# Two left half passes in every segment, and left output rows placed from scratch memory

## The chip, the core and the metric

The kernel runs on one core of a Trainium2 chip. A core has a matrix engine (TensorE, PE), a vector engine (VectorE, DVE), a scalar engine (ScalarE, ACT), a general engine (GpSimd, POOL) and an engine that mainly issues transfers (SyncE, SP). They run side by side and meet through semaphores. Sixteen DMA engines move data between the chip's main memory (HBM) and the on-chip memory, and work off what SP and POOL issue. TensorE writes its sums into accumulator banks, which another engine empties. The metric is device time in microseconds (us), lower is better.

## What is computed

Two branches work on the same layer-normed input and are added to it: a recurrent attention with memory (A), and a dense layer with GELU (B). Sizes: 2048 rows of 1024; 32 heads of 128; segments of 32 rows, so 64 segments; 8 memory rows; hidden width 3584.

```python
def _A_ref(x, mem0, Wq, Wk, Wv, Wo, seg_len):
    ...
    for s in range(n_seg):
        xs = x[:, s * seg_len:(s + 1) * seg_len, :].copy()
        h = jnp.concatenate([mem, xs], axis=1)
        q = jnp.einsum('btd,dhe->bhte', h, Wq)
        k = jnp.einsum('btd,dhe->bhte', h, Wk)
        v = jnp.einsum('btd,dhe->bhte', h, Wv)
        scores = jnp.einsum('bhqe,bhke->bhqk', q, k) * scale
        scores = jnp.where(mask[None, None], scores, -1000000000.0)
        p = _softmax(scores, axis=-1)
        o = jnp.einsum('bhqk,bhke->bhqe', p, v)
        o = jnp.einsum('bhte,hed->btd', o, Wo)
        mem = o[:, :M, :].copy()
        outs.append(o[:, M:, :])
    return jnp.concatenate(outs, axis=1)
...
xn = _layernorm(x, axis=-1)
return x + _A_ref(xn, A_mem0, A_Wq, A_Wk, A_Wv, A_Wo, A_seg_len) + _B_ref(xn, B_w1, B_b1, B_w2, B_b2)
```

The first 8 output rows of a segment are the memory rows of the next one, so the 64 segments run one after another, and each uses all of Wq, Wk, Wv and Wo.

## The kernel before

**First part.** For four blocks of 512 rows the kernel does the layer norm, the dense layer and the sum with x (lines 214 to 453). The sum, R_n, goes to main memory; turn_R (L309) rearranges it there into hr_d (for each segment) and hrL_d (for each group of four), in the layout in which the attention output will come. The normed rows go there too, transposed, in columns 0 to 255 of the same two tensors.

**Main rows and left rows.** A product with a weight uses at most 32 rows at a time. Of the 40 rows of a segment, 8 memory rows and the first NX = 24 rows of x are the main rows. The other NL = 8 are the left rows. As they don't depend on the recurrence until the attention, the left rows of four segments (GRP = 4, a group) are put together to 32 and go through the weights once for each group. In segment s, g, i4 = divmod(s, GRP).

**Weights.** Wq, Wk, Wv and Wo are cut into 64 units of 128 x 2048 elements, 512 KB each. 43 stay in on-chip memory; 21, spread evenly over the order of use, are fetched again in each segment (IS_STREAMED, "the stream"). They go through STREAM_BUFS = 6 buffers on SP's queue: start_stream (L182) issues the next transfer, and is called by unit_done (L480) when a streamed unit has been used; the transfer waits until TensorE has read the buffer. unit_done also hands one or two of the waiting small transfers (the list named small) to POOL's queue.

**A segment** (L508 to L787) is a fixed order of half passes. half_pass (L526) multiplies eight units of K, Q or V (u = 0 or 1, half of the heads) with the main rows into an accumulator, and, if asked (left), with the left rows into a second one, psL. Dictionaries named at say after which unit other work is done: turning keys and queries (turn_k, turn_q, and turn_kL, turn_qL for left rows), scores, sums (the softmax denominators) and values. The order is K0, Q0, V0, K1, Q1, V1, then the output product with 16 units of Wo (o_product, L672), where a left output product from the tiles oL goes into psXL. There are three accumulator banks in turn, named acc. K0 is called with lead=3: products of left rows with up to three resident units come before the first main product.

Before, the left half passes stand so: K0, K1 and V1 in segments with i4 = 0; none with i4 = 1; Q0 and Q1 with i4 = 2; V0 and the output product with i4 = 3 (left_k, left_q, left_v and left_o, lines 518 to 521). The output product takes as many matrix instructions as two half passes. Values VL[u] of left rows, keys kL[u] and queries qL are kept over the segments of a group; qS (L703) keeps the queries for the last segment while qL is written for the next group.

**End of a segment.** ScalarE copies the output sum to o_sb (L768). put_mem (L204) turns it on TensorE, and VectorE copies the 8 memory columns into the next segment's hT (L208). On VectorE the order is: with i4 = 3, resL = psXL + resL (L771); then the memory copy L208; then res = psX + res (L774). res and resL come by POOL from hr_d and hrL_d after unit 7 of the output product (L762, L765). Four stores of res (L778) and, with i4 = 3, 16 stores of resL (L785) are appended to small. The softmax tile pr and res share one piece of on-chip memory (tag "e"), resL shares one with VL[1] (tag "VL1").

**Queues.** [...] On POOL these are, for a segment: hr for the next segment (L194, waits until TensorE has used the present one, after V1), res, resL, then the stores. SP has the stream alone once the first segment has started.

Of the kernel before, what the change touches and what calls it, by code (L numbers as in the profile page):

```python
# [10 lines left out]
BF16 = mybir.dt.bfloat16  # L11
# [5 lines left out]
P = 128  # L17
# [6 lines left out]
SEG = 32  # L24
MEM = 8
NSEG = S // SEG
# [9 lines left out]
NX = 24  # L36
NL = SEG - NX
# [36 lines left out]
def kernel(  # L74
# [34 lines left out]
    hr_d = dram.tile([NSEG + 1, P, 512], BF16, name="hr_d")  # L109
    hrL_d = dram.tile([NGRP + 1, P, 512], BF16, name="hrL_d")  # L110
    R_n = dram.tile([S, DM], BF16, name="R_n")

    slabs = ctx.enter_context(tc.tile_pool(name="slabs", bufs=1))
    consts = ctx.enter_context(tc.tile_pool(name="consts", bufs=1))
# [100 lines left out]
    with tc.tile_pool(name="ma", bufs=2) as ma, tc.tile_pool(name="mps", bufs=6, space=PSUM) as mps:  # L215
# [93 lines left out]
        def turn_R(ttg, small=None):  # L309

            for i in range(4):
                rows = R_n[ttg * P + i * SEG:ttg * P + (i + 1) * SEG, :].rearrange("t (j c) -> t j c", j=4)
                dst = hr_d[4 * ttg + i + 1, :, 256:512].rearrange("(j t) c -> t j c", j=4)
                dstL = hrL_d[ttg + 1, :, 256:512].rearrange("(j t) c -> t j c", j=4)[NL * i:NL * i + NL, :, :]
                for o, r in ((dst, rows), (dstL, rows[NX:SEG, :, :])):
                    if small is None:
                        nc.sync.dma_start(out=o, in_=r)
                    else:
                        small.append(lambda o=o, r=r: nc.gpsimd.dma_start(out=o, in_=r))
# [140 lines left out]
    with tc.tile_pool(name="late", bufs=1) as late, \  # L460
# [43 lines left out]

        hT, hL = nxt["hT"], nxt["hL"]
        qL = qlp.tile([P, 8, P], BF16, name="qL")
        kL, VL, oL = [None] * 2, [None] * 2, [None] * 2
        for s in range(NSEG):  # L508
            g, i4 = divmod(s, GRP)
            first, final = s == 0, s + 1 == NSEG  # L510
# [3 lines left out]
                small.appendleft(lambda g=g: load_left_rows(g + 1, nc.gpsimd))  # L514


            more = g + 1 < NGRP
            left_k = i4 == 0
            left_q = first or (i4 == 2 and more)
            left_v = first or (i4 == 3 and more), i4 == 0  # L520
            left_o = i4 == 3
            if left_q and not first:
                hL = nxt["hL"]
            st = {}
# [37 lines left out]
            def left_out(psL, tag, pool=sp):  # L562
                nat = pool.tile([P, 512], BF16, name="natL", tag=tag)
                nc.vector.tensor_copy(out=nat[:, :], in_=psL[:, :])  # L564
                return nat

            def turn_k(nat):
                tr = trp.tile([P, 4, P], BF16, name="tr")
# [16 lines left out]
            def turn_qL(nat, u):  # L585
                turn4(nat, qL[:, 4 * u:4 * u + 4, :])

            def q_left(u):

                if i4 == 3 and more:  # L590
                    q = qS[:, u, :, :]
                else:
                    q = by_head(qL[:, 4 * u:4 * u + 4, :])[:, :, NL * i4:NL * i4 + NL]
                nc.vector.tensor_copy(out=st["qT"][:, :, 32:40], in_=q)
# [51 lines left out]
            def values(u, r):  # L646

                V, prA, prB = st["V"], st["prA"], st["prB"]
                av = avp.tile([P, 2, 512], F32, name="av")
                oV = av[:, :, 0:160].rearrange("p b (c q) -> p b c q", q=40)  # L650
                for c in range(4):
                    for b in range(2):
                        q = slice(64 * r + 32 * b, 64 * r + 32 * b + 32)
                        nc.tensor.matmul(  # L654
                            oV[:, b, c, :], lhsT=V[q, c * P:(c + 1) * P], rhs=prA[q, c, :],
                            start=(c == 0), stop=False, skip_group_check=True, tile_position=(64 * r + 32 * b, 0),
                        )
                    for b in range(2):
                        q = slice(64 * r + 32 * b, 64 * r + 32 * b + 32)
                        nc.tensor.matmul(  # L660
                            oV[:, b, c, NX:40], lhsT=VL[u][q, c * P:(c + 1) * P], rhs=prB[q, c, :],
                            start=False, stop=True, skip_group_check=True, tile_position=(64 * r + 32 * b, 0),
                        )
                if r == 0:
                    st["oT", u] = sp.tile([P, 4, 4, 32], BF16, name="oT", tag="db"[u])
                    if i4 == 0:
                        oL[u] = late.tile([P, 4, 4, 32], BF16, name=f"oL{u}")
                cp = nc.vector.tensor_copy if r else nc.scalar.copy
                cp(out=st["oT", u][:, 2 * r:2 * r + 2, :, :], in_=oV[:, :, :, 0:32])  # L669
                cp(out=oL[u][:, 2 * r:2 * r + 2, :, NL * i4:NL * i4 + NL], in_=oV[:, :, :, 32:40])  # L670

            def o_product(unit, t, lhs, acc, seq):  # L672
                w, i, u = unit
# [22 lines left out]
                at[2].append(lambda: q_left(0))  # L696
            if left_q:
                at[2].append(lambda: st.update(natL=left_out(psQL, "d")))
                at[5] = [lambda: turn_qL(st["natL"], 0)]
                if first:  # L700
                    at[5].append(lambda: q_left(0))
                else:
                    qS = sp.tile([P, 2, 16, NL], BF16, name="qS")  # L703
                    at[5].insert(0, lambda: keep_q(0))
            psV, psVL = half_pass("V", 0, left_v[0], at)
            st["V"] = left_out(psV, "b")
            if first:
                VL[0] = left_out(psVL, "VL0", late)


            psK1, psK1L = half_pass("K", 1, left_k, {1: [sums]})
            natk1 = rows_out(psK1, "d")
            at = {2: [lambda: turn_k(natk1)], 4: [lambda: values(0, 0)], 6: [lambda: values(0, 1)]}
            if left_k:
                at[2].append(lambda: st.update(natL=left_out(psK1L, "d")))
                at[4].insert(0, lambda: turn_kL(st["natL"], 1))
            psQ1, psQ1L = half_pass("Q", 1, left_q, at)
            natq1 = rows_out(psQ1, "b")
            if left_v[0] and not first:
                VL[0] = left_out(psVL, "VL0", late)  # L720
            at = {3: [lambda: turn_q(natq1)], 6: [lambda: scores(1)]}
            if first:
                at[3].append(lambda: st.update(natL=left_out(psQ1L, "VL1", late)))
# [3 lines left out]
            if left_o:  # L727
                psXL = accp.tile([P, 512], F32, name="acc")

                def o_lefts(k):
                    for unit in O_LEFT[k]:
                        o_product(unit, unit_tile(unit), oL, psXL, O_LEFT_SEQ)

                at.setdefault(1, []).append(lambda: o_lefts(0))
            psV1, psV1L = half_pass("V", 1, left_v[1], at)
            st["V"] = left_out(psV1, "a")
            if left_v[1]:
                VL[1] = left_out(psV1L, "VL1", late)  # L740
            if not final:
                load_x_rows(s + 1, nc.gpsimd)


            at = {1: [sums], 4: [lambda: values(1, 0)], 6: [lambda: values(1, 1)]}
            if left_q and not first:
                at[7] = [lambda: keep_q(1)]
                at[8] = [lambda: st.update(natL=left_out(psQ1L, "d"))]
                at[11] = [lambda: turn_qL(st["natL"], 1)]
            psX = accp.tile([P, 512], F32, name="acc")  # L750
            resL = None
            for n, unit in enumerate(O_UNITS):
                t = unit_tile(unit)
                o_product(unit, t, [st["oT", 0], st.get(("oT", 1))], psX, O_UNITS)
                if left_o and unit in O_LEFT[1]:
                    o_product(unit, t, oL, psXL, O_LEFT_SEQ)
                unit_done(unit)
                for fn in at.get(n, ()):
                    fn()
                if n == 7:  # L760
                    res = sp.tile([P, 256], BF16, name="res", tag="e")
                    nc.gpsimd.dma_start(out=res[:, :], in_=hr_d[s + 1, :, 256:512])  # L762
                    if left_o:
                        resL = late.tile([P, 256], BF16, name="resL", tag="VL1")
                        nc.gpsimd.dma_start(out=resL[:, :], in_=hrL_d[g + 1, :, 256:512])  # L765
            if not final:
                o_sb = sp.tile([P, 256], BF16, name="o_sb", tag="d")
                nc.scalar.copy(out=o_sb[:, :], in_=psX[:, 0:256])  # L768
            if left_o:
                o_lefts(2)  # L770
                nc.vector.tensor_tensor(out=resL[:, :], in0=psXL[:, 0:256], in1=resL[:, :], op=ALU.add)  # L771
            if not final:
                put_mem(o_sb, nxt["hT"], trp.tile([P, 4, P], BF16, name="tr"))
            nc.vector.tensor_tensor(out=res[:, :], in0=psX[:, 0:256], in1=res[:, :], op=ALU.add)  # L774

            for jq in range(4):
                o = out_flat[s * SEG:s * SEG + NX, 256 * jq:256 * jq + 256]
                small.append(lambda o=o, r=res[32 * jq:32 * jq + NX, :]: nc.gpsimd.dma_start(out=o, in_=r))  # L778
            if left_o:
                rows_o = out_flat[g * GRP * SEG:(g + 1) * GRP * SEG, :].rearrange("(i t) d -> i t d", t=SEG)  # L780
                for jq in range(4):
                    for i in range(GRP):
                        o = rows_o[i, NX:SEG, 256 * jq:256 * jq + 256]
                        r = resL[32 * jq + NL * i:32 * jq + NL * i + NL, :]
                        small.append(lambda o=o, r=r: nc.gpsimd.dma_start(out=o, in_=r))  # L785
            if not final:
                hT = nxt["hT"]  # L787
# [35 lines left out]
```

The softmax here doesn't subtract the row's maximum and nothing guards it: scores larger than these inputs give would overflow.

## Time and profile before

| What | us |
|---|---|
| Runs (four): lowest, median, highest | 2338.39, 2346.52, 2351.84 |
| The profiled execution, its own time | 2338.39 |
| Its span in the trace | 2336.6 |
| TensorE busy (share of the span) | 2023.7 (87%) |
| VectorE busy | 699.0 (30%) |
| ScalarE busy | 517.3 (22%) |
| POOL busy | 372.7 (16%) |
| First o_sb copy (end of segment 0) begins | 472.3 |
| Last o_sb copy (end of segment 62) begins | 2285.9 |

The profiled execution is the fastest of the four runs. Its span is 1.8 us shorter than its time. Busy shares are means over unlike stages: the first part is 420 us of matrix work with little traffic, and the 64 segments after it move 512 KB units all the time. The queue of SP moved 769.66 MB in all, that of POOL 15.92 MB. In the chain of waits that ended last, 50% of the span is TensorE and 40% is transfers, most of these the stream: 24% waiting for units of Wq, 5% each for Wo and Wv, 3% for Wk.

Among the transfers of POOL, res takes 5.2 us from issue to landing in the median, the stores of res 5.2 us and of resL 5.4 us, hr 5.5 us, resL 5.1 us. A stream unit takes 6.6 to 7.4 us, of which several are under way at once.

### The profile page before, as it was taken

How to read it: one execution, taken by the hardware profiler on the slowest of the kernel's cores; microseconds unless marked ns; L12 is line 12 of the kernel's file. 1: busy time of each engine (PE TensorE's matmuls, PEld its weight loads, DVE VectorE, ACT ScalarE, POOL GpSimd, SP SyncE). 2: the span in 40 equal slices, each digit the busy share in tenths (PEclk: the TensorE clock that was granted, in tenths of full speed). 3: DMA queues.
4: the chain of work that ended last, by engine and by line, in shares of the span. 5: the costliest groups of instructions: out<-in, count | busy, mean ns of one | idle time of the engine just before them, and what ended most of it. 6: DMA issues, size and time to landing. Idle time of an engine off the chain costs nothing.

```text
span 2336.6 us, 84620 instructions
## 1 busy us (share of the span) xinstructions
PE 2023.7 (87%) x37779; PEld 1046.7 (45%) x37779; DVE 699.0 (30%) x1922; ACT 517.3 (22%) x1221; POOL 372.7 (16%) x745
## 2 busy tenths in 40 slices
PE   7999999788888888888888888888888888888885
PEld 3444444344444444444444444444444444444443
DVE  6574753122222222222222222222222222222221
ACT  5261432121212121211121111111212121111121
POOL 0000000023121212121212121212121212121212
PEclk9999999999999999999999999999999999999998
DMA  9521126899999999999999999999999999999995
GB/s 322 192 68 47 39 66 257 328 403 380 405 378 397 380 397 377 405 378 380 368 405 369 395 376 404 376 404 378 404 378 400 376 400 358 399 371 396 373 402 225
DMA packets 266409, 792.03 MB, mean 339 GB/s; under 512 B 55995, under 2 KB 71131, under 8 KB 266044
## 3 DMA queue, kind: packets, MB, share of 16 engines
q1 hardware_dynamic: 243004, 769.66, 85.4%
q0 software_dynamic: 22464, 15.92, 2.2%
q8 instruction: 295, 4.83, 0.8%
q10 hardware_dynamic: 576, 1.05, 0.1%
q14 instruction: 70, 0.57, 0.1%
HBM read 772.83 MB, written 29.88 MB: 344 GB/s over the span
## 4 chain that ended last, share of the span: by engine, by line
PE 50%; DMA 40%; issue 4%; DVE 3%; ACT 2%; POOL 1%; DVEq 0%; ACTq 0%; POOLq 0%; SPq 0%
DMA u<-Wc_Q 24%; PE acc L536 17%; PE ps L358 8%; PE acc L676 8%; PE ps L405 6%; DMA u<-Wc_O 5%; DMA u<-Wc_V 5%; DMA u<-Wc_K 3%; PE av L654 2%; PE tr L493 2%; DMA resL<-hrL_d 2%; PE ps L438 2%; PE av L660 1%; DMA res<-hr_d 1%; DVE natL L564 1%
## 5 line engine op out<-in xcount | busy, mean ns | idle before, releaser
L536 PE MATMUL acc<-u,hr 128*32 128x512 bf16 x12288 | 952.1, 384 | 133.9 <-DMA u<-Wc_Q 63.7
L536 PEld LDWEIGHTS <-hr 128*32 128x32 bf16 x12288 | 314.5, 96 | 471.6 <-issue 222.8
L536 PE MATMUL acc<-u,hrL 128*32 128x512 bf16 x3072 | 299.7, 381 | 4.0 <-ACT xtok L451 1.1
L559 ACT CAST nat<-acc 128x512 bf16<-128x512 f32 x256 | 150.1, 586 | 544.5 <-PE acc L536 506.2
L676 PEld LDWEIGHTS <-oT 128*32 128x32 bf16 x8192 | 208.6, 97 | 96.7 <-issue 76.8
L676 PE MATMUL acc<-u,oT 128*32 128x256 bf16 x4096 | 187.5, 275 | 22.8 <-DMA u<-Wc_O 11.2
L564 DVE CAST natL<-acc 128x512 bf16<-128x512 f32 x224 | 152.5, 687 | 173.3 <-PE acc L536 173.3
L676 PE MATMUL acc<-W_O,oT 128*32 128x256 bf16 x4096 | 173.3, 277 | 31.1 <-issue 31.0
L358 PE MATMUL ps<-u 128*128 128x512 bf16 x896 | 195.4, 381 | 2.6 <-ACT u L282 2.6
L194 POOL DMA_DIRECT2D hr<-hr_d x63 | 34.9, 555 | 1005.3 <-PE acc L536 585.2
L778 POOL DMA_DIRECT2D out_dram<-res x256 | 129.4, 512 | 359.7 <-DVE res L774 356.6
L571 DVE COPY kT<-tr 128x512 bf16<-128x512 bf16 x128 | 54.4, 425 | 325.9 <-PE tr L493 325.9
L405 PE MATMUL ps<-u 128*128 128x512 bf16 x672 | 147.0, 379 | 0.0
L358 PEld LDWEIGHTS <-u 128*128 128x128 bf16 x896 | 88.0, 98 | 108.7 <-issue 4.2
L785 POOL DMA_DIRECT2D out_dram<-resL x256 | 128.0, 505 | 52.5 <-DMA out_dram<-resL 22.5
L628 ACT ACTIVATE pr<-sm 128x224 bf16<-128x224 f32 x128 | 45.8, 358 | 402.6 <-PE sm L623 351.3
L583 DVE COPY qT<-tr 128x512 bf16<-128x512 bf16 x128 | 54.4, 425 | 265.6 <-PE tr L493 265.6
L654 PEld LDWEIGHTS <-natL 32*128 32x128 bf16 x2048 | 78.4, 91 | 84.7 <-issue 50.7
L669 DVE CAST oT<-av 128x256 bf16<-128x256 f32 x128 | 54.4, 425 | 200.6 <-PE av L660 198.6
L536 PEld LDWEIGHTS <-hrL 128*32 128x32 bf16 x3072 | 84.2, 96 | 65.3 <-issue 11.0
L654 PE MATMUL av<-pr,natL 32*128 32x40 bf16 x2048 | 94.8, 177 | 17.7 <-DVE pr L642 8.9
L493 PEld LDWEIGHTS <-nat 128*128 128x128 bf16 x1024 | 57.9, 98 | 104.9 <-issue 61.0
(100 smaller groups left out, 1806.1 us busy)
## 6 DMA issues: line engine op xcount, KB each, us to landing
u<-Wc_K SPq DMA_DIRECT2D x384, 512.0 KB, 6.9
u<-Wc_Q SPq DMA_DIRECT2D x384, 512.0 KB, 7.4
u<-Wc_O SPq DMA_DIRECT2D x320, 512.0 KB, 7.2
u<-Wc_V SPq DMA_DIRECT2D x256, 512.0 KB, 6.6
u<-in_B_w_dram SPq DMA_DIRECT2D x16, 448.0 KB, 5.7
u<-in_B_w_dram SPq DMA_DIRECT2D x14, 512.0 KB, 10.8
u<-in_A_Wv_dram SPq DMA_DIRECT2D x12, 512.0 KB, 7.9
u<-in_A_Wk_dram SPq DMA_DIRECT2D x10, 512.0 KB
```

Source lines behind the costliest of these rows:

```text
L358: nc.tensor.matmul(ps[:, :].rearrange("p (s t) -> p s t", t=SEG), lhsT=w1_sb[fb // 14 * 8 + kt][:, (fb % 14) * P:(fb % 14 + 1) * P], rhs=x ...
L405: nc.tensor.matmul(ps[:, :], lhsT=gts[fc // 4][:, fc % 4, t * P:(t + 1) * P], rhs=w2_sb[fc // 2][:, fc % 2, cs], start=(fc == 0), stop=(fc ...
L493: nc.tensor.transpose(dst[:, c, :], nat[:, c * P:(c + 1) * P], ident[:, :])
L536: nc.tensor.matmul(acc[32 * j:32 * j + 32, :], lhsT=lhs[:, i, :], rhs=t[:, 512 * j:512 * j + 512], start=(i == seq[0]), stop=(i == seq[-1] ...
L559: nc.scalar.copy(out=nat[:, :], in_=ps[:, :])
L564: nc.vector.tensor_copy(out=nat[:, :], in_=psL[:, :])
L571: nc.vector.tensor_copy(out=st["kT"][:, :, :], in_=by_head(tr[:, :, :]))
L583: nc.vector.tensor_copy(out=st["qT"][:, :, 0:32], in_=by_head(tr[:, :, :]))
L654: nc.tensor.matmul(oV[:, b, c, :], lhsT=V[q, c * P:(c + 1) * P], rhs=prA[q, c, :], start=(c == 0), stop=False, skip_group_check=True, tile ...
L676: nc.tensor.matmul(acc[32 * jq:32 * jq + 32, 0:256], lhsT=lhs[i // 4][:, i % 4, 2 * u + k, :], rhs=t[:, 1024 * k + 256 * jq:1024 * k + 256 ...
L778: small.append(lambda o=o, r=res[32 * jq:32 * jq + NX, :]: nc.gpsimd.dma_start(out=o, in_=r))
L785: small.append(lambda o=o, r=r: nc.gpsimd.dma_start(out=o, in_=r))
```

## The change

Left output rows are now collected over other segments than the left inputs. og, slot = divmod(s + 2, GRP), so the left output product is made in segments with i4 = 1 for the segments s - 3 to s (and in the last segment for the last two); V1 of the left rows moves to i4 = 3. The count of left half passes becomes two in each: K0, K1; output; Q0, Q1; V0, V1. There are 17 left output products, as the first covers segments 0 and 1 alone and the last 62 and 63. The tiles oL are allocated and cleared once before the loop. turn_R puts the left rows of R_n into the new group and slot, and for the first and last two segments into a second slot as well. resL is loaded in V1 and has the tag of qS. The stores of res are issued at the end of the segment, not through small. The left output rows are stored once to outL_d in main memory, and from there one transfer for each segment of the group puts them into the output.

```diff
+    outL_d = dram.tile([NGRP + 1, P, 256], BF16, name="outL_d")
...
         def turn_R(ttg, small=None):
             for i in range(4):
-                rows = R_n[ttg * P + i * SEG:ttg * P + (i + 1) * SEG, :].rearrange("t (j c) -> t j c", j=4)
-                dst = hr_d[4 * ttg + i + 1, :, 256:512].rearrange("(j t) c -> t j c", j=4)
-                dstL = hrL_d[ttg + 1, :, 256:512].rearrange("(j t) c -> t j c", j=4)[NL * i:NL * i + NL, :, :]
-                for o, r in ((dst, rows), (dstL, rows[NX:SEG, :, :])):
+                seg = 4 * ttg + i
+                rows = R_n[seg * SEG:(seg + 1) * SEG, :].rearrange("t (j c) -> t j c", j=4)
+                pairs = [(hr_d[seg + 1, :, 256:512].rearrange("(j t) c -> t j c", j=4), rows)]
+                og, slot = divmod(seg + 2, GRP)
+                for sl in (slot, slot ^ 2) if seg in (0, 1, NSEG - 2, NSEG - 1) else (slot,):
+                    dst = hrL_d[og, :, 256:512].rearrange("(j t) c -> t j c", j=4)[NL * sl:NL * sl + NL, :, :]
+                    pairs.append((dst, rows[NX:SEG, :, :]))
+                for o, r in pairs:
...
-        kL, VL, oL = [None] * 2, [None] * 2, [None] * 2
+        kL, VL = [None] * 2, [None] * 2
+        oL = [late.tile([P, 4, 4, 32], BF16, name=f"oL{u}") for u in range(2)]
+        for t in oL:
+            nc.vector.memset(t[:, :, :, :], 0.0)
...
-            left_v = first or (i4 == 3 and more), i4 == 0
-            left_o = i4 == 3
+            left_v = first or (i4 == 3 and more)
+            left_o = i4 == 1 or final
+            og, slot = divmod(s + 2, GRP)
...
+            def left_values(u, ps):
+                VL[u] = left_out(ps, f"VL{u}", late)
...
-                    if i4 == 0:
-                        oL[u] = late.tile([P, 4, 4, 32], BF16, name=f"oL{u}")
-                cp(out=oL[u][:, 2 * r:2 * r + 2, :, NL * i4:NL * i4 + NL], in_=oV[:, :, :, 32:40])
+                cp(out=oL[u][:, 2 * r:2 * r + 2, :, NL * slot:NL * slot + NL], in_=oV[:, :, :, 32:40])
...
-                at[5] = [lambda: turn_qL(st["natL"], 0)]
                 if first:
-                    at[5].append(lambda: q_left(0))
-                else:
-                    qS = sp.tile([P, 2, 16, NL], BF16, name="qS")
-                    at[5].insert(0, lambda: keep_q(0))
-            psV, psVL = half_pass("V", 0, left_v[0], at)
+                    at[5] = [lambda: turn_qL(st["natL"], 0), lambda: q_left(0)]
+            psV, psVL = half_pass("V", 0, left_v, at)
             if first:
-                VL[0] = left_out(psVL, "VL0", late)
-            psK1, psK1L = half_pass("K", 1, left_k, {1: [sums]})
+                left_values(0, psVL)
+            at = {1: [sums]}
+            if left_q and not first:
+                qS = sp.tile([P, 2, 16, NL], BF16, name="qS")
+                at[3] = [lambda: keep_q(0)]
+                at[5] = [lambda: turn_qL(st["natL"], 0)]
+            psK1, psK1L = half_pass("K", 1, left_k, at)
...
+            if left_v and not first:
+                at[6].append(lambda: left_values(0, psVL))
             psQ1, psQ1L = half_pass("Q", 1, left_q, at)
-            if left_v[0] and not first:
-                VL[0] = left_out(psVL, "VL0", late)
...
+                def load_resL():
+                    st["resL"] = sp.tile([P, 256], BF16, name="resL", tag="qS")
+                    nc.gpsimd.dma_start(out=st["resL"][:, :], in_=hrL_d[og, :, 256:512])
                 at.setdefault(1, []).append(lambda: o_lefts(0))
-            psV1, psV1L = half_pass("V", 1, left_v[1], at)
+                at[3].append(load_resL)
+            psV1, psV1L = half_pass("V", 1, left_v, at)
             st["V"] = left_out(psV1, "a")
-            if left_v[1]:
-                VL[1] = left_out(psV1L, "VL1", late)
+            if first:
+                left_values(1, psV1L)
...
             at = {1: [sums], 4: [lambda: values(1, 0)], 6: [lambda: values(1, 1)]}
+            if left_v and not first:
+                at[6].append(lambda: left_values(1, psV1L))
...
-                    if left_o:
-                        resL = late.tile([P, 256], BF16, name="resL", tag="VL1")
-                        nc.gpsimd.dma_start(out=resL[:, :], in_=hrL_d[g + 1, :, 256:512])
...
             for jq in range(4):
-                o = out_flat[s * SEG:s * SEG + NX, 256 * jq:256 * jq + 256]
-                small.append(lambda o=o, r=res[32 * jq:32 * jq + NX, :]: nc.gpsimd.dma_start(out=o, in_=r))
+                cs = slice(256 * jq, 256 * jq + 256)
+                nc.gpsimd.dma_start(out=out_flat[s * SEG:s * SEG + NX, cs], in_=res[32 * jq:32 * jq + NX, :])
             if left_o:
-                rows_o = out_flat[g * GRP * SEG:(g + 1) * GRP * SEG, :].rearrange("(i t) d -> i t d", t=SEG)
-                for jq in range(4):
-                    for i in range(GRP):
-                        o = rows_o[i, NX:SEG, 256 * jq:256 * jq + 256]
-                        r = resL[32 * jq + NL * i:32 * jq + NL * i + NL, :]
+                nc.gpsimd.dma_start(out=outL_d[og, :, :], in_=resL[:, :])
+                for sl in range(GRP):
+                    row = (GRP * og - 2 + sl) * SEG + NX
+                    if s - GRP < row // SEG <= s and row >= 0:
+                        o = out_flat[row:row + NL, :].rearrange("t (j c) -> t j c", j=4)
+                        r = outL_d[og, :, :].rearrange("(j t) c -> t j c", j=4)[NL * sl:NL * sl + NL, :, :]
                         small.append(lambda o=o, r=r: nc.gpsimd.dma_start(out=o, in_=r))
```

More of the change, by code (lines that the diff above doesn't have):

```diff
@@ L750 @@
             psX = accp.tile([P, 512], F32, name="acc")
-            resL = None
             for n, unit in enumerate(O_UNITS):
@@ L770 @@
                 o_lefts(2)
+                resL = st["resL"]
                 nc.vector.tensor_tensor(out=resL[:, :], in0=psXL[:, 0:256], in1=resL[:, :], op=ALU.add)
```

## The prediction

> **What bounds the kernel now.** I read the page first, then the busy times and bandwidth of each recurrent segment, then the stretches around the segment boundaries, then who waits there. From the page, the slices in time:
>
> ```profile
> DMA  9521126899999999999999999999999999999995
> GB/s 322 192 68 47 39 66 257 328 403 380 405 378 397 380 397 377 405 378 380 368 405 369 395 376 404 376 404 378 404 378 400 376 400 358 399 371 396 373 402 225
> ```
>
> From the ninth slice on, the 64 recurrent segments run, the transfer engines are 90% busy or more, and the bandwidth swings between about 404 and 376. A slice is 58.4 us, about two segments, so the swing has the period of a group of four segments: two of them run at about 404 and two lose something. Cut at the end of each segment (the end of the o_sb copy, L768), one group, segments 24 to 27, reads as follows (from:to, length, busy us of PE, PEld, DVE, ACT and POOL, clock, DMA share, GB/s):
>
> ```profile
> 1147.66:1176.53 28.87, 26.22 (x591) 13.88 (x580) 8.86 (x24) 5.56 (x16) 11.62 (x23) 1.00 0.94 354
> 1176.53:1204.31 27.78, 22.50 (x476) 11.20 (x476) 5.98 (x18) 5.56 (x16) 3.12 (x6) 1.00 1.03 404
> 1204.31:1232.98 28.67, 25.34 (x548) 13.03 (x548) 7.44 (x22) 5.56 (x16) 3.11 (x6) 1.00 1.02 404
> 1232.98:1263.24 30.26, 26.29 (x636) 15.32 (x636) 6.52 (x19) 5.56 (x16) 3.63 (x7) 1.00 1.01 386
> ```
>
> I call the four kinds by i4, which counts the segments of a group: kind 0 has three left half passes (K0, K1, V1), kind 1 none, kind 2 two (Q0, Q1), kind 3 V0 and the left output product, worth two, so three. Kinds 1 and 2 run at 404 GB/s whether they carry no left half pass or two: the stream of weights sets their length, and two half passes cost nothing. Kinds 0 and 3, with three, fall to 354 and 386. Added up over 13 groups (segments 8 to 59) with the same view, the means are 29.44, 28.18, 28.41 and 31.23 us at 358, 401, 400 and 388 GB/s; a group takes 117.25 us and moves 45.3 MB. Where in the segments the rate is lost, around a boundary from kind 3 to kind 0 (first two rows) and one from 0 to 1, 1 to 2 and 2 to 3 (the others):
>
> ```profile
> 1258.24:1263.24 5.00, 5.00 (x191) 4.60 (x189) 0.56 (x2) 0.86 (x3) 1.07 (x2) 1.00 0.97 345
> 1263.24:1268.24 5.00, 2.79 (x56) 1.15 (x50) 0.85 (x3) 0.00 (x1) 1.00 (x2) 1.00 0.67 234
> 1295.58:1300.58 5.00, 4.17 (x66) 1.97 (x67) 1.04 (x3) 0.59 (x2) 2.02 (x4) 1.00 0.96 345
> 1323.77:1328.77 5.00, 4.66 (x78) 2.27 (x82) 0.93 (x3) 0.59 (x1) 2.02 (x4) 1.00 1.03 401
> 1351.81:1356.81 5.00, 4.07 (x66) 2.01 (x67) 1.04 (x3) 0.59 (x2) 2.02 (x4) 1.00 0.99 370
> ```
>
> The hole is the 3-to-0 boundary: over 13 groups the first 5 us of kind 0 average 223 GB/s against 380 to 392 for the others, and the last 5 us of kind 3 average 339 against about 400. Why the stream stops there is seen in the timeline of the SP queue, of TensorE and of VectorE:
>
> ```profile
> 1259.34 3.19 SPq L186 DMA_DIRECT2D u<-Wc_Q  x3
> 1267.34 1.36 SPq L186 DMA_DIRECT2D u<-Wc_V  x2
> ```
> ```profile
> 1263.63 0.83 PE L536 MATMUL acc<-u,hrL 128*32 128x512 bf16 x12
> 1266.67 0.40 PE L536 MATMUL acc<-u,hr 128*32 128x512 bf16 x4 [2.21 <-DVE hr L208]
> ```
> ```profile
> 1266.10 0.42 DVE L771 TENSOR_TENSOR resL<-acc,resL 128x256 bf16<-128x256 f32 x1 [5.91 <-DMA resL<-hrL_d]
> 1266.44 0.18 DVE L208 COPY hr<-tr 128x64 bf16<-128x64 bf16 x1
> ```
>
> SP issues no stream transfer for 4.8 us (1262.53 to 1267.34), because all six buffers hold weights that TensorE has not used. TensorE is late for two reasons: it had the left output product in the segment before, and now the left K product; and it waits 2.21 us for the memory columns (L208), which stand on VectorE behind the resL addition, which waits for a load issued late. That last wait totals 64.2 us in 11 of 16 groups.
>
> [...] The trace agrees in kind: it holds 400 to 404 over whole segments, so I take 400 as the ceiling of this kernel. [...] In this trace a POOL transfer takes 5.1 to 5.6 us to land beside the stream, 1.5 at the least. [...]
>
> **The change part by part.**
> 1. *Two left half passes in each segment.* V1 goes from kind 0 to kind 3, the output product from kind 3 to kind 1. The number of products in a group is the same, so this is worth the stalls alone. At 400 GB/s kind 0 loses 29.44 x (400 - 358)/400 = 3.09 us and kind 3 loses 31.23 x (400 - 388)/400 = 0.94 us, together 4.03 us; the same from the bytes: 117.25 - 45.3 MB/400 GB/s = 4.0. There are 15 such boundaries: 60 us. What is late next is the stream. I check that the two new boundaries stay inside the six buffers (21 of 64 units are streamed, 1.3 us each). A left unit costs 0.216 us of TensorE (the step between such matmul groups in the trace). Kind 1 gets 16 of them, 3.5 us, where TensorE is busy 22.6 of 28.2 us; kind 3 gives two half passes away and gets V1, kind 0 drops V1. No boundary has left O and left K in a row any more. I leave 0.3 us in each for what the 370 and 345 rows show of ordinary boundaries: 15 x 0.3 = +4.5 us.
> 2. *resL loaded in V1 (at[3]) from its own slot.* Issued on POOL over 7 us before its use, against a median landing of 5.1 us: the wait of L771 goes. It is part of the hole in step 1 and isn't counted again. The addition, 0.42 us, still stands ahead of the memory copy, now in kind 1; the stream hides it.
> 3. *Left rows through scratch.* For each group 16 POOL stores of 505 ns become one store and four DRAM-to-DRAM transfers of about as long: 8.1 to 2.5 us of POOL, which bounds nothing. The bytes grow by 64 KB a group: 0.16 us at 400 GB/s, 16 x 0.16 = +2.6 us. The first of the four waits for the scratch store to land, some 6 us; behind it stand three like it, then the hr load, wanted only after V1, about 20 us later. DRAM-to-DRAM isn't in this part of the trace at these sizes; [...]
> 4. *res stores straight after the addition.* Before, POOL's queue already held them next (L778 waits on L774), so the order is the same outside the first five segments: nothing.
> 5. *keep_q(0) and turn_qL(0) from V0 to K1; left V copies into Q1 and the O part.* keep_q now reuses resL's slot and waits until the scratch store has landed: four res stores end some 6 us into the segment, plus 0.5 and 5.4, so 12 us, and keep_q is due at about 13. Zero, up to 1 us if late; VectorE's next copy is 3 us off. In kind 3, V1's accumulator is the one of psVL, whose 0.69 us copy now follows the oT and oL copies (0.42 and 0.21): TensorE waits about 1.1 us at V1. Where the stream sets the pace this lies in the buffers: zero, up to 1.1 us a group, 18 us, if not.
> 6. *oL cleared first, once.* Two memsets on VectorE wait until the last rows stored from the memory they take over have landed, 432.8 us (R_n, on the chain of waits). The kT copy of 429.5 is then 4 us late, the left K transposes 3.3 us; but TensorE waits anyway at 433.0 to 440.4 for the first streamed V. Zero, at most 3.3 us.
> 7. *One left output product more* (17, as segments 0 and 1 make one): 16 x 0.216 = 3.5 us of TensorE in segment 1, under the stream. Zero, at most 3.5.
> 8. *The tail.* From the POOL timeline:
>
> ```profile
> 2312.35 0.55 POOL L762 DMA_DIRECT2D res<-hr_d  x1 [20.65 <-DVE oT L669]
> 2312.89 0.54 POOL L765 DMA_DIRECT2D resL<-hrL_d  x1
> 2317.88 2.02 POOL L778 DMA_DIRECT2D out_dram<-res  x4 [4.45 <-DVE res L774]
> 2319.89 7.95 POOL L785 DMA_DIRECT2D out_dram<-resL  x16
> ```
>
> The span ends at 2336.6, 8.8 us after the last issue. After: the additions end 0.6 us sooner (no wait for resL), four stores to 2319.3, the scratch store to 2319.8, landed at about 3.4 us more (as the resL load here) 2323.2, two transfers to 2324.2, plus 8.8: 2333.0, so -3.6 us (2 to 5).
>
> Sum: -60 + 4.5 + 2.6 - 3.6 = -56.5 us. The profiled execution took 2338.39 us (span 2336.6 and 1.8 around it): 2282. It is the lowest of the four runs; the median lies 8.1 higher, and from it the change gives 2290. A median is what will be compared, so I take 2288.
>
> **The rivals.**
> *The hole moves rather than closes* (faster, by less). For it: the left output product ends kind 1 with three left units and an addition before the memory copy, and the left K product follows three left half passes of kind 3 units. Against: the 2-to-3 boundary with two half passes behind it runs at 370, not 234. If half the hole stays: 30 us off, less 1, so 2346.5 - 29, about 2318.
> *Nothing changes.* The stream might not hold 400 when every segment draws at full rate, if the fast kinds only use what the slow ones leave. Against: both fast kinds hold it for 56 us in a row. Time 2344.
> *Slower: TensorE with its waits is the bound, and accumulators run out.* Then moved products gain nothing, and what counts is the stalls added: 1.1 us at V1 of kind 3 (psVL's bank) and 0.7 us behind the resL addition and keep_q, 1.8 us a group, 29 us: 2375. It decides only if stalls of TensorE can't be made up from the buffers, that is, if it has no slack in kinds 1 and 2; their waits for the stream (3.2 us per segment of kind 1) speak against it.
>
> **How the numbers follow.** Forecast 0.72, half the hole 0.14, no change 0.06, slower 0.08. The range goes from the whole hole with a ceiling of 404 (another 1.1 us a group, 17 us, taken off the lower base, 2266) to just beyond half the hole (2322), and leaves out the last two cases. About 0.5%, 12 us, is what a measurement can tell from no change here: faster 0.86, same 0.06, slower 0.08.
>
> **What would show it.** Right: all four kinds within 28 to 29 us at 395 GB/s or more; the first 5 us of kind 0 above 350; no wait of the resL addition on its load; the last SP gap over 2 us gone; a tail 3 us shorter. Wrong: a stretch under 300 GB/s at the 1-to-2 or 3-to-0 boundary, TensorE waiting for a natL copy at V1 with the stream idle, or segments of one length but at 390 GB/s or less.

## The result, and the profile after

The changed kernel takes 2347.08 us in the median of 43 runs (2334.8 to 2367.06), the kernel before 2346.19 us in 64 (2333.94 to 2357.57). The ratio is 1.0007, with a 95% interval of 0.9996 to 1.0019: no difference. The profiled execution of the changed kernel has a span of 2351.7 us at a mean granted clock of 0.98, that of before 2336.6 us at 0.99. As the medians are equal, these 15 us are no property of the change, and I compare the two traces for where time goes, not for its total.

From the page of the changed kernel, the slices and one queue (packets, MB, share of 16 engines):

```profile
DMA  9521126999999999999999999999999999999997
GB/s 323 188 68 49 37 79 251 340 377 404 376 384 383 401 362 398 385 395 379 379 381 385 368 402 388 388 366 388 375 382 367 392 383 396 355 385 381 393 367 297
q8 instruction: 296, 4.85, 0.8%
```

The swing between 404 and 376 is gone, but not upwards: most slices lie between 366 and 396. A group cut at the ends of the o_sb copies, segments 16 to 19, kinds 0 to 3 in order (columns as in the prediction):

```profile
917.92:945.07 27.15, 25.01 (x548) 13.26 (x548) 8.02 (x22) 5.56 (x15) 3.11 (x6) 1.00 1.02 399
945.07:977.43 32.36, 25.08 (x604) 14.56 (x604) 5.98 (x18) 5.56 (x15) 4.16 (x8) 1.00 1.00 393
977.43:1004.74 27.31, 25.13 (x558) 12.89 (x548) 7.68 (x23) 5.56 (x15) 5.89 (x11) 1.00 0.99 375
1004.74:1034.49 29.75, 25.05 (x540) 12.82 (x540) 7.11 (x20) 5.56 (x15) 3.16 (x6) 1.00 1.03 403
```

Every kind now has left work that the change counts as two half passes, and 25 us of TensorE, and still kind 1, which got the left output product, takes 32.36 us. The last 5 us of kind 1 and the first 5 of kind 2:

```profile
972.43:977.43 5.00, 3.31 (x121) 2.97 (x112) 0.05 (x1) 0.37 (x1) 0.52 (x1) 1.00 0.88 332
977.43:982.43 5.00, 4.60 (x88) 2.10 (x82) 0.99 (x4) 0.59 (x1) 2.56 (x5) 1.00 0.89 274
```

The hole has moved with the left output product from the 3-to-0 to the 1-to-2 boundary. Over 13 groups (segments 8 to 59) the last 5 us of kind 1 average 328 GB/s and the first 5 of kind 2 average 247; before, the pair at 3-to-0 was 339 and 223. A group takes 118.41 us (117.25 before). In the first of the two windows TensorE is busy 3.31 of 5 us although its units are there. Its timeline shows what the prediction had read as plain matrix work:

```profile
968.71 0.28 PE L689 MATMUL acc<-u,oT 128*32 128x256 bf16 x2
970.14 0.40 PE L689 MATMUL acc<-u,oT 128*32 128x256 bf16 x6 [1.15 <-issue]
...
973.57 0.28 PE L689 MATMUL acc<-W_O,oL 128*32 128x256 bf16 x2
975.53 0.40 PE L689 MATMUL acc<-W_O,oL 128*32 128x256 bf16 x6 [1.69 <-issue]
```

TensorE stops in the middle of a unit, between its second and third matmul, for 1.15 and 1.69 us, although the operands have been there since the first. "issue" means that the profile shows nothing that it waited for. I call these stops supply gaps, and count those where over 0.55 us pass between two matmul starts and no instruction between has a wait. In 13 groups there are 55 (44 before), 6.0 us a group (4.1 before), the largest part in the kind with the left output product (2.8; 2.1 before). Three facts of the trace say what they are. All of them fall at the same place in every 256 of TensorE's instructions, matmuls and weight loads counted together: 193 to 195 after a multiple of 256, 55 of 55 and 44 of 44. Queue 8 moves packets of 16 KB, 296 of them, and 4.85 MB over 75,886 instructions of TensorE is 64 bytes for each, so a packet holds 256. And nine in ten gaps end between 1.29 and 1.60 us after the end of such a packet, while the packets follow each other at 6.4 us in the median. I read this as TensorE having run out of instructions; the experiments test it.

The other steps, in the waits, and in POOL's tail:

```profile
DVE resL L789 <- PE acc L689: 96.8, 17, 7.4
PE acc L689 <- issue: 62.6, 47, 2.8
```
```profile
2341.83 2.02 POOL L796 DMA_DIRECT2D out_dram<-res  x4 [3.86 <-DVE res L792]
2343.84 0.56 POOL L799 DMA_DIRECT2D outL_d<-resL  x1
2345.95 1.13 POOL L805 DMA_DIRECT2D out_dram<-outL_d  x2 [1.55 <-DMA outL_d<-resL]
```

The resL addition waits for TensorE alone now, never for its load. The tail from TensorE's end to the span's is 11.0 us against 20.7.

### The profile page after: what moved, and what is told of

The parts are those of the page before. It is cut to its first block, busy times and chain, and to the rows that moved or that the text cites. A ratio compares the mean times of both kernels' runs of the same rounds, so it can differ in the third digit from the quotient of the medians.

```text
span 2351.7 us, 84626 instructions
## 1 busy us (share of the span) xinstructions
PE 2036.6 (87%) x37907; PEld 1059.6 (45%) x37907; DVE 699.6 (30%) x1925; ACT 517.4 (22%) x1221; POOL 291.7 (12%) x573
## 3 DMA queue, kind: packets, MB, share of 16 engines
q8 instruction: 296, 4.85, 0.8%
## 4 chain that ended last, share of the span: by engine, by line
PE 56%; DMA 32%; issue 6%; DVE 3%; ACT 2%; POOL 1%; DVEq 0%; ACTq 0%; POOLq 0%; SPq 0%
PE acc L548 20%; DMA u<-Wc_Q 19%; PE acc L689 11%; PE ps L363 8%; PE ps L410 6%; DMA u<-Wc_V 4%; DMA u<-Wc_O 3%; PE av L669 2%; PE tr L498 2%; DMA res<-hr_d 2%; DMA out_dram<-res 2%; DMA u<-Wc_K 2%; PE ps L443 2%; PE av L675 1%; DVE pr L657 1%
## 5 line engine op out<-in xcount | busy, mean ns | idle before, releaser
L689 PEld LDWEIGHTS <-oT 128*32 128x32 bf16 x8192 | 213.6, 99 | 90.1 <-issue 64.5
L689 PE MATMUL acc<-W_O,oT 128*32 128x256 bf16 x4096 | 181.9, 289 | 30.2 <-issue 30.1
L498 PE MATMUL tr<-ident,nat 128*128 128x128 bf16 x1024 | 102.1, 222 | 0.4 <-ACT nat L571 0.3
```

Source lines behind the costliest of these rows:

```text
L498: nc.tensor.transpose(dst[:, c, :], nat[:, c * P:(c + 1) * P], ident[:, :])
L689: nc.tensor.matmul(acc[32 * jq:32 * jq + 32, 0:256], lhsT=lhs[i // 4][:, i % 4, 2 * u + k, :], rhs=t[:, 1024 * k + 256 * jq:1024 * k + 256 ...
```

## Experiments

All ratios are to the kernel before, run beside it on the same chip. "Gaps" are supply gaps; the bandwidth is of the last 5 us of the kind with the left output product and of the first 5 us after it. Gaps, bandwidth and group time are from one profiled execution each, 13 groups.

| Run | Ratio, 95% interval | Gaps, us a group | GB/s | Group, us |
|---|---|---|---|---|
| before | 1 | 4.1 | 339, 223 | 117.25 |
| changed | 1.0007 (0.9996-1.0019) | 6.0 | 328, 247 | 118.41 |
| a_half_instr | 0.9922 (0.9901-0.9943) | 4.4 | 396, 304 | 116.22 |
| a_half_cols | 0.9999 (0.9976-1.0022) | 6.5 | 347, 256 | 117.77 |
| a_no_left_o | 0.9814 (0.9784-0.9845) | 3.4 | 398, 385 | 114.86 |
| b_half_instr | 0.9898 (0.9870-0.9927) | 3.1 | 385, 223 | 116.18 |
| a_double_instr | 1.0217 (1.0182-1.0252) | 7.9 | 252, 198 | 121.06 |
| a_split_v | 0.9985 (0.9971-1.0000) | 5.1 | 358, 273 | 116.65 |
| a_main_half | 0.9718 (0.9686-0.9750) | 0.06 | 392, 389 | 113.72 |
| b_early_resL | 0.9991 (0.9969-1.0013) | 5.1 | 337, 241 | 116.79 |
| b_main_half | 0.9957 (0.9939-0.9975) | 0 | 396, 275 | 116.74 |
| b_main_half_early2 | 0.9749 (0.9711-0.9787) | 0 | 391, 375 | 113.25 |
| a_left_sum | 0.9971 (0.9956-0.9986) | 4.7 | 396, 303 | 117.92 |
| a_sum2 | 0.9729 (0.9706-0.9752) | 0 | 401, 393 | 114.17 |

The theory (I) is that the supply of instructions makes the hole; the rival (W), which was the prediction's own reading, that the matrix work of the left output product does.

**Same work, half the instructions; same instructions, half the work.** A unit of the output product takes two heads. Eight matmuls of 256 columns can be four of 512, if each head has two of the four partition blocks:

```diff
             def o_product(unit, t, lhs, acc, seq):
...
                 for k in range(2):
                     for jq in range(4):
                         nc.tensor.matmul(
                             acc[32 * jq:32 * jq + 32, 0:256],
                             lhsT=lhs[i // 4][:, i % 4, 2 * u + k, :],
                             rhs=t[:, 1024 * k + 256 * jq:1024 * k + 256 * jq + 256],
...
+                def o_left(unit, t):
...
+                    for j in range(4):
+                        nc.tensor.matmul(
+                            psXL[32 * j:32 * j + 32, 0:512],
+                            lhsT=oL[i // 4][:, i % 4, 2 * u + j // 2, :],
+                            rhs=t[:, 512 * j:512 * j + 512],
...
-                        o_product(unit, unit_tile(unit), oL, psXL, O_LEFT_SEQ)
+                        o_left(unit, unit_tile(unit))
```

The main product keeps o_product. The sums of the two heads stay apart and are not added up.

> Changed kernel, but each unit of the left output product is four matmuls of 512 columns and not eight of 256: the same TensorE columns, half the instructions. The two heads' partial sums land in separate partition blocks and aren't added up, so the left output rows aren't the reference's. Theory I (TensorE runs out of instructions in the left output product: 256 of them last 3.5 us there, and a refill doesn't come faster): the gaps without a releaser in kind 1 fall from 2.8 us a group to about 1.5, the 1-to-2 hole shrinks, 20 to 40 us faster than before. Theory W (the 3.5 us of matrix work is what six buffers can't bridge): the time of before within 5 us, hole as it was.

> Kernel before, with the left output product as four matmuls of 512 columns for each unit: same TensorE columns, half the instructions, partial sums not added up, so the left output rows aren't the reference's. Theory I: the 3-to-0 hole shrinks, 15 to 35 us faster than before. Theory W: within 5 us of before.

Against it, the eight matmuls with 128 columns each (rhs ends at + 128, so that half the columns of the left rows are left out):

> Changed kernel, but each matmul of the left output product takes 128 columns and not 256: the same number of instructions, half the TensorE work. Half of the columns of the left output rows are left out (and not added). Theory I: at most 10 us faster than before, hole still under 300 GB/s. Theory W: half the hole goes, about 30 us faster.

Halving the instructions gave 18 us in the changed kernel (0.8% of 2346) and 24 in the one before; halving the work gave nothing. W falls. A fixed cost of every matmul inside TensorE, another reading of these runs, isn't it either: where the left units run without a stop, one takes 0.216 us with four matmuls, 0.219 with eight, and 0.112 with eight of half the columns (medians of the step to the next unit). The size in the changed kernel is just under what was expected. In the kernel before, kind 3's end recovers to 385, but the first 5 us after it stay at 223: something else sits there too. The resL addition waits 86.3 us for its load in that run, against 64.2 before; the runs with the load in V1 take this up below.

**Twice the instructions, in the output product and elsewhere.** The left output product as sixteen matmuls of 128 columns; and, in the other run, each matmul of the left V products of kind 3 as two of 256. In this order:

```diff
+                        for c in (0, 128):
+                            for jq in range(4):
+                                nc.tensor.matmul(
+                                    psXL[32 * jq:32 * jq + 32, c:c + 128],
...
-                            acc[32 * j:32 * j + 32, :],
+                            acc[32 * j:32 * j + 32, c:c + n],
```

> Changed kernel, with the left output product as sixteen matmuls of 128 columns for each unit: the same TensorE columns and results, twice the instructions. Theory I: gaps in kind 1 rise from 2.8 us a group to 5 or more, 25 to 60 us slower than before. Theory W: within 5 us of the changed kernel.

> Changed kernel, with each matmul of the left V products of kind 3 split into two of 256 columns: the same TensorE columns and results, twice the instructions (64 more matmuls and weight loads a segment for each half pass would be 128; here 64). Theory I: gaps without a releaser appear in V0 and V1 of kind 3 (now 0.9 us a group in that kind, then over 2), bandwidth around the 3-to-0 boundary falls, 8 to 30 us slower. Theory W: within 4 us of the changed kernel.

The first was slower by 51 us, within theory I's 25 to 60, with 4.7 us of gaps in kind 1 and this boundary (windows as above, 5 us before and after the end of kind 1):

```profile
985.55:990.55 5.00, 2.77 (x154) 2.62 (x143) 0.00 (x0) 0.37 (x1) 0.00 (x0) 1.00 0.90 317
990.55:995.55 5.00, 4.60 (x91) 2.16 (x83) 0.98 (x4) 0.58 (x1) 2.56 (x5) 1.00 0.57 179
```

The second was not slower: theory I's expectation for it missed, and W's, within 4 us of the changed kernel, came close (0.9985 against 1.0007, 5 us). Gaps in kind 3 did rise, from 0.9 to 1.7 us a group, but they fell in kinds 0 and 2, and their sum didn't rise (5.1 against 6.0). Nor are those of kind 3 the split V's own: all 21 follow a block of 256 instructions with at least 50 matmuls of the main output product. The 20 blocks with 40 or more of the left V, and no semaphore wait at their end, took 5.2 to 7.8 us, as transposes and attention stand among them, and none was followed by a stop of over 0.21 us. So this run didn't make its stage dense enough to test the theory there.

How dense is too dense? A main and a left unit together take 0.432 us. Worked out from that, with 32 instructions for the two (the output product) 256 of them last 3.46 us, with 48 (doubled) 2.3 us. Cut into blocks at the ends of the packets' 256 instructions, the traces show how long TensorE took for a block, and how many of these blocks were followed by a supply gap (blocks that end in a wait for a semaphore are left out; a_main_half is described below):

| Block took, us | before | changed | a_double_instr | a_main_half |
|---|---|---|---|---|
| under 3.6 | 5 of 5 | 11 of 11 | 31 of 31 | none |
| 3.6 to 4.8 | 31 of 45 | 33 of 39 | 19 of 37 | none |
| 4.8 to 6.0 | 7 of 36 | 11 of 45 | 11 of 39 | 1 of 33 |
| over 6.0 | 0 of 70 | 0 of 65 | 0 of 63 | 0 of 88 |

There is no sharp limit: in these four traces a gap always follows under 3.6 us and never over 6. A block with its gap takes 5.4 to 5.7 us in the median of the first three traces. Why some blocks of 4 us get through isn't shown.

**Without the left output product.** 13 of its 16 units left out (O_LEFT keeps its last list only):

> Changed kernel, with 13 of the 16 units of the left output product left out, so the left output rows aren't the reference's. Both theories: the 1-to-2 hole closes, all four kinds within 29 us, about 55 to 65 us faster than before. A third theory (the resL addition ahead of the memory copy, or the scratch stores, make the hole): the hole stays and the time is within 15 us of before.

The hole closes and the time falls by 44 us, less than the 55 to 65 expected: gaps of 3.4 us a group remain. The third theory falls: resL's addition and the scratch stores are all there, and no hole.

**Half the instructions in the main product too.**

> Changed kernel, with the main output product and the left one as four matmuls of 512 columns for each unit: the same TensorE columns, half the instructions of the whole output stage. Partial sums aren't added up, so all output rows are not the reference's. Theory I: the gaps without a releaser fall below 2 us a group (6.0 before), the 1-to-2 hole closes, 40 to 60 us faster than before. Rival (what is left of the hole after halving the left product alone is matrix work): no more than the 18 us that that run gave.

It gave 66 us (2.8%), above the 40 to 60 expected and more than leaving the left product out. No block of 256 instructions takes under 4.8 us now (table above). One group, kinds 0 to 3:

```profile
906.47:933.56 27.09, 24.86 (x484) 11.25 (x484) 8.02 (x22) 5.56 (x16) 3.11 (x6) 1.00 1.02 406
933.56:963.11 29.55, 25.00 (x476) 11.11 (x476) 5.98 (x18) 5.56 (x15) 4.16 (x8) 1.00 1.03 405
963.11:990.85 27.74, 25.35 (x490) 11.49 (x484) 7.77 (x23) 5.56 (x15) 5.89 (x11) 1.00 1.02 402
990.85:1019.14 28.29, 24.41 (x476) 11.22 (x476) 7.12 (x20) 5.56 (x15) 3.17 (x6) 1.00 1.02 400
```

All four kinds run at 400 GB/s or more here, and at 397 to 400 in the mean of 13 groups. TensorE's busy time is as before, and the mean group takes 113.7 us, close to the 113.2 that the prediction had put down to the even spread.

**One part alone: the early load of resL.**

```diff
+                def load_resL():
+                    st["resL"] = sp.tile([P, 256], BF16, name="resL", tag="qS")
+                    nc.gpsimd.dma_start(out=st["resL"][:, :], in_=hrL_d[g + 1, :, 256:512])
...
+                at[3].append(load_resL)
```

> Kernel before, with resL loaded in V1 into the slot of qS: one part of the change alone. If the late resL load was a cause of the 3-to-0 hole as the prediction had it: the wait of L771 goes, the first 5 us of kind 0 rise from 223 to 300 GB/s or more, 10 to 30 us faster. If the instruction supply alone sets the pace there: within 5 us of before.

The wait for the load is gone from the trace, and the time is unchanged, with the hole at 337 and 241.

**Both causes in the kernel before.** First the halved instructions without the early load, then with it:

> Kernel before, with the main and the left output product as four matmuls of 512 columns for each unit (partial sums not added, so the output rows aren't the reference's). If the prediction's idea holds once TensorE has its instructions (an even spread of left half passes is worth something): clearly slower than the changed kernel with the same edit, 2295 to 2315 against 2278. If the spread is worth nothing and the supply was all of it: within 6 us of 2278 but for the longer tail, 2280 to 2292.

> Kernel before, with both output products as four matmuls of 512 columns for each unit (partial sums not added, so the output rows aren't the reference's) and resL loaded in V1 as in the changed kernel; left half passes stay 3, 0, 2, 3. If the late resL load is what held the run without it at 2336: the wait of 2.7 us a group goes and the time falls to 2285 to 2300. What then remains above 2278, less about 9 us of tail, is the worth of the even spread: above 2300 it is worth something once TensorE has its instructions, at 2285 to 2292 nothing. If the late load isn't the cause: 2330 or more.

The first outcome fitted neither guess: 0.9957, far from 0.9718, without a single supply gap. VectorE's timeline at a 3-to-0 boundary, and the total in the waits:

```profile
1036.45 0.42 DVE L769 TENSOR_TENSOR resL<-acc,resL 128x256 bf16<-128x256 f32 x1 [6.26 <-DMA resL<-hrL_d]
1036.79 0.18 DVE L208 COPY hr<-tr 128x64 bf16<-128x64 bf16 x1
```
```profile
DVE resL L769 <- DMA resL<-hrL_d: 95.5, 15, 7.2
```

With its instructions in time, TensorE ends the output stage sooner, the load after unit 7 comes later still against it, and the memory columns wait behind the addition: 95.5 us in all, 64.2 before. That order of events is read from the timeline; the next run tests it. With the load early as well, 0.9749. So in the kernel before two causes lie over each other at one boundary, and taking away either alone gives 24 us or less, but both give 59 (2.5%). The interval of this run overlaps that of a_main_half; the medians' ratios differ by 0.3%, some 7 us, and the tails of the two profiles by 19.8 - 11.0 = 8.8 us. The even spread itself (2, 2, 2, 2 against 3, 0, 2, 3) is worth nothing that these runs can tell.

**A version that computes all rows.** First only the left product, the two heads' sums added on VectorE in four additions after the memory copy; then both products, the sums added on TensorE by slices of the identity:

```diff
+        def add_halves(ps, part):
...
+                    nc.tensor.matmul(
+                        ps[64 * ch:64 * ch + 64, 0:256], lhsT=ident[:, 64 * k:64 * k + 64],
+                        rhs=part[:, 256 * ch:256 * ch + 256], start=(k == 0), stop=(k == 1), tile_position=(0, 64 * ch),
```

> Changed kernel, with the left output product as four matmuls of 512 columns for each unit and the two heads' partial sums added on VectorE, in four additions of 256 columns after the memory copy, so that the left rows are computed in full. 10 to 20 us faster than before, as the run without the additions (18 us); if the four additions hold up an accumulator or the res stores, less than 8.

> Changed kernel, with both output products as four matmuls of 512 columns, and the two heads' partial sums added on TensorE (matmuls with slices of the identity) after ScalarE has copied them, so that all rows are computed in full. 40 to 60 us faster than before, against 69 for the run without the additions; less than 25 if the longer way to the memory columns (a copy of 512 columns, eight small matmuls for two transposes) isn't hidden by the buffers.

The first kept 7 us of the 18: the additions come ahead of the res addition, its stores land later, and pr waits for them (138.2 us in total; 72.8 without the additions). The second takes 2280.99 us, ratio 0.9729, and beats the kernel before, and with it the changed one, by 63 us, just above the 40 to 60 expected. No supply gap is left in its 13 groups, and its page reads, over the segments, as the prediction had wanted:

```profile
GB/s 325 200 50 56 53 45 212 307 400 404 403 382 394 401 401 401 403 400 397 362 401 396 399 395 399 396 402 399 403 394 400 392 405 398 397 397 406 397 406 296
```

## Why the prediction was wrong

- **The ceiling and the size of the hole: right.** 400 GB/s can be held through all kinds, and a closed hole is worth about 4 us a group: 113.72 and 113.25 us were reached against 113.2 worked out. (Beside the hole, the last 5 us of kind 0 averaged 377 GB/s before, not about 400 as the others.)
- **Step 1, what makes the hole: wrong, and this is the step that failed.** It said that no boundary would have the left output and the left K product in a row any more, that a left unit of the output product costs 0.216 us of TensorE, and that the 3.5 us that kind 1 gets stay inside the six buffers. The 0.216 us is right for a unit that runs (0.219 measured). The sum lacked the supply of instructions, which it left out without a reason: in this stage TensorE uses up 256 of them in 3.46 us by the 0.432 us measured for a main and a left unit, and after the 11 blocks that took under 3.6 us it stopped for 2.1 us on average. So the count of half passes, by which the work was spread, was the wrong measure. "The output product takes as many matrix instructions as two half passes", says the section on the kernel before, and that is wrong: it takes about as much time (0.219 us for a left unit, 0.225 for one of a half pass), but 128 matmuls against 64. The prediction's own rows show it, x548 for kind 2 with two left half passes and x636 for kind 3 with one and the left output product. The stops were in the profile of before as well:

```profile
PE acc L676 <- issue: 49.2, 43, 2.2
q8 instruction: 295, 4.83, 0.8%
```

- **Step 2, the late load: half right.** The wait went, as forecast. But it was one of two causes, and it paid nothing as long as the other stood (0.9991). The prediction had put it under step 1 and so didn't ask what would be late next. The addition still stands ahead of the memory copy, and waits for TensorE: in 5 of the 16 segments of kind 1 the memory columns are there only 1.4 to 3.7 us after the o_sb copy (0.8 to 1.0 in the others). In a_main_half, without the stops, it is 0.8 to 0.9 in all 16.
- **Steps 3 and 4: right as far as seen.** No run isolates the scratch transfers, but a_main_half has them all and shows no loss.
- **Step 5: right in effect.** With the supply repaired, neither the waits for V1's accumulator nor keep_q cost bandwidth in kind 3 that shows (398 GB/s over 13 groups of a_main_half).
- **Step 6: right.** The memsets began at 434.49 us and the kT copy came 5.4 us late, not 4; TensorE waited 5.05 us for the left K rows, and the o_sb copy of segment 0 came 0.4 us sooner than before:

```profile
434.49 0.55 DVE L516 MEMSET oL<- 128x256 uint32 x2 [11.65 <-issue]
434.95 0.36 DVE L586 COPY kT<-tr 128x512 bf16<-128x512 bf16 x1
```

- **Step 7, one left output product more: open.** No run isolates it.
- **Step 8, the tail: right, but mis-sized.** 9.7 us, not 3.6. The last issue is followed by 4.6 us and not by 8.8, and the scratch store landed in 1.55 us after its issue, not 3.4.
- **The sum.** From the median it comes to 2290; why 2288 was taken isn't said.
- **The rivals.** "The hole moves" was named with half its size, 0.14, and a wrong reason (three units and an addition). It moved whole. "Nothing changes" has the right time by luck: its reason (the stream can't hold 400) is refuted by a_main_half and a_sum2. "Slower" didn't come.

So where did the 60 us go? The hole was not closed but carried along by the left output product, with 1.9 us a group more of supply gaps in the profiled run, and as the medians are equal, the 9.7 us gained in the tail must have been lost in the segments. Why the gaps grew isn't shown. My guess, which no run tests, is that an edit shifts where the blocks of 256 end; 44 of the 50 that took under 4.8 us in the changed kernel, 36 of 50 before, were followed by a gap. The changed kernel's profiled execution also ran 96 us at half clock, the one before 49. Over the 44 executions of the changed kernel the time is about 17 us longer for each 0.01 that the mean granted clock is lower (a straight line through them, correlation -0.78), and 0.01 is what the two profiles differ by. So the 15 us between the spans, and part of the 1.2 us between the groups, go with the clock.

## What to carry to other kernels

Before work is spread over stages to even them out, take a stage's cost in all the things that it uses up, instructions included: here 256 of them in under 4.8 us were followed by a stop in 44 of 50 cases (changed kernel), and wider matmuls, not fewer columns, were the cure. The stops of TensorE between two matmuls of one unit, with "issue" as the releaser, were not noise here: all 55 of the changed kernel fell at the same place in every 256 instructions. Check such stops against the packets of the instruction queue. And when a single cause is removed and nothing happens, remove the second one as well before calling the first harmless: 0.9991 and 0.9957 alone were 0.9749 together.

## What the hardware showed beyond that

- Equal columns weren't equal time for this kernel: four matmuls of 512 columns for eight of 256 in the output stage took 2.8% off the whole, with TensorE's busy time at 25 us a segment in both.
- The supply gaps ended 1.2 to 1.6 us after the packet of 256 instructions had been moved (476 of the 478 gaps in the eleven traces that have any), and the packet itself took about 1.06 us (median) beside the stream.
- The packets of 256 instructions didn't come closer than 3.4 us in the traces of before, changed and a_double_instr, although the doubled product, by the 2.3 us worked out above, would use them up faster.
- Repairing one wait lengthened another: the late load cost 64.2 us before and 95.5 us once TensorE had its instructions.
